# Attention in cross-shaped windows on one core: the kernel without the nine warming matmuls ahead of the first transposes

## The chip, the cores and the metric

The kernel runs on one NeuronCore of a Trainium2 chip. The metric is the device time of one execution in microseconds (us), the median of several runs; lower is better. The five engines are called as in the profile: PE (matrix multiply, with PEld for its weight loads), ACT (activation functions), DVE (vector), POOL (general purpose) and SP (it issues most transfers).

## The reference

The input is an image of 224 x 224 pixels with 96 channels. It is projected to q, k and v. The first 48 channels attend within horizontal stripes of 8 rows, the last 48 within vertical stripes of 8 columns, so there are 28 + 28 stripes of 1792 pixels each. The two halves are put side by side and projected once more.

```
qkv = einsum('bhwc,cd->bhwd', x, wqkv)            # 96 -> 3 * 96
ah  = softmax(einsum('bqc,bkc->bqk', qh, kh) * 48 ** -0.5)   # per horizontal stripe, 1792 x 1792
oh  = einsum('bqk,bkc->bqc', ah, vh)
av, ov = the same for the vertical stripes
o   = concat(oh, ov) over channels
return einsum('bhwc,cd->bhwd', o, wo)
```

## The kernel before

**Tiling.** Two stripes are worked on at a time; such a pair is called P, and there are 28 of them, 14 horizontal and 14 vertical. A pair has 4 query chunks (512, 512, 512 and 256 queries) and 14 key tiles of 128 keys. One unit of work is one chunk against one key tile for both stripes (two key tiles for the chunk of 256): PE writes 128 x 1024 scores into two PSUM banks (line 1015, `qk_op`), one engine turns them into exponentials, and PE multiplies these with V into the chunk's output (line 968, `pv_op`). Two matmuls that stand next to each other there use different parts of the array and run side by side, so matmuls are counted in pairs below.

**Who makes the exponentials.** Most units go to ACT: one activation of 128 x 1024 (line 1037), 1071 of them. The others go to DVE and POOL, which build the exponential from integer operations (lines 1075, 1088, 1090 and 1094).

**The order of the work.** Each engine has queues of operations, and the order in which a queue is served is written out by hand: `PLAN` holds one digit for each operation, and the digit names the queue that is served next. Digit 0 on PE is the queue `q_first`, the start of the kernel. Waits are semaphore waits that the planner puts ahead of an operation; every engine works its own list from first to last.

**The start**, which is where the change lies:

- ACT issues the transfer of the second stripe of pair 0 in natural layout (line 502, `x_nat`, into `Ph_sb`, which serves as scratch there), and then that of the weights `w_sb` (line 509). SP issues the transfer of the first stripe, transposed on its way (line 504, `x_tr`), and two more transposing ones for pair 1 (line 558).
- DVE clears `warm` (line 507) and other buffers and builds an identity matrix in `Ph_sb` (lines 513 to 521).
- PE runs `NWARM` matmuls of zeros (line 532): weights 128 x 128 and 512 columns, both from `warm`, into banks 0 to 3. Nobody reads the result. They wait for the clearing of `warm` alone.
- PE transposes the second stripe by 16 matmuls against the identity (line 647, `x_turn`, in four groups of four, numbered 0 to 3). DVE copies groups 0 and 2 to `xT_sb`, ACT groups 1 and 3 (line 652).
- PE projects K in four pieces (line 686) and Q of chunk 0 (lines 686 and 679); ACT and DVE copy them out (lines 705, 706 and 699), DVE adds up the sums of K and subtracts the mean (lines 713 and 719). PE then projects most of V (line 761) and Q of chunk 1, and starts the first scores (line 1015), for which it needs Q of chunk 0 and the first 256 keys from line 719. The first exponential on ACT follows.

The warming matmuls:

```
        for i in range(NWARM):
            first("pe", 0.427, lambda e, i=i: e.matmul(bank(i % 4)[:, :], lhsT=warm[:, 0:128], rhs=warm[:, :],
                                                       start=True, stop=True), [o_warm], mode="v")
```

## Time and profile before

| | |
|---|---|
| Median of 3 runs | 1008.08 us (1004.94 to 1011.19) |
| The profiled execution's own time | 1004.3 us |
| Its span, first to last instruction | 1002.5 us |
| ACT busy in it | 987.6 us (99%) |
| PE busy in it | 988.0 us (99%) |
| DVE and POOL busy in it | 938.5 us (94%) and 684.2 us (68%) |

Times within the profile are counted from the start of the span. The busy share of PE needs care: matmuls are pipelined and their ends are modelled, so that a PE shown as busy isn't necessarily at its peak. The clock column of the profile (PEclk) is the share of full speed that was granted to PE; what it says of the first microseconds is looked at below.

### The profile page before, as it was taken

What the parts mean: (1) busy time and instruction counts of PE and PEld (TensorE: products, weight loads), DVE (VectorE), ACT (ScalarE), POOL (GpSimd) and SP (SyncE); (2) the same over time, 40 slices, a digit from 0 to 9 for tenths busy, and PEclk for the clock granted to TensorE, in tenths of its full rate; (3) what the DMA queues carried; (4) which work ended last, traced back from release to release, by engine and by line L of the source; (5) the groups of instructions that cost most, each with busy time, mean ns of one, the idle gap of its engine ahead of it and who ended that gap; (6) DMA issues with size and microseconds to landing.
All of it is one profiled execution on the core that took longest, in us unless ns stands there. A gap on an engine that the chain in (4) does not pass through costs nothing.

```text
span 1002.5 us, 24560 instructions
## 1 busy us (share of the span) xinstructions
PE 988.0 (99%) x10211; PEld 385.9 (38%) x10211; DVE 938.5 (94%) x1573; ACT 987.6 (99%) x1080; POOL 684.2 (68%) x660
## 2 busy tenths in 40 slices
PE   8999999999999999999999999999999999999997
PEld 3433433343343334334334333433433443343342
DVE  8999999999999999999899999999999999999997
ACT  7999999999999999999999999999999999999997
POOL 3676766667677676777776776776676777677652
PEclk9999999999999999999999999999999999999999
DMA  5102120220112023011111122222122221222012
GB/s 110 39 2 38 38 32 8 38 38 1 39 39 32 8 38 38 2 36 25 27 29 32 25 46 50 54 52 44 34 41 52 53 54 39 52 52 40 13 36 50
DMA packets 164712, 36.92 MB, mean 37 GB/s; under 512 B 164488, under 2 KB 164488, under 8 KB 164600
## 3 DMA queue, kind: packets, MB, share of 16 engines
q1 hardware_dynamic: 163016, 34.80, 18.5%
q8 instruction: 80, 1.31, 0.5%
q10 hardware_dynamic: 1584, 0.55, 0.2%
q14 instruction: 32, 0.26, 0.1%
HBM read 0.44 MB, written 9.63 MB: 10 GB/s over the span
## 4 chain that ended last, share of the span: by engine, by line
ACT 70%; PE 29%; DVE 1%; issue 0%
ACT PT L1037 70%; PE ps L968 13%; PE ps L1015 11%; PE ps L686 2%; PE ps L761 1%; PE ps L843 1%; PE ps L532 0%; PE ps L809 0%; DVE OT_sb L931 0%; PE ps L647 0%; DVE out_sb L866 0%; DVE I_sb L1075 0%; DVE E_sb L1090 0%; DVE U_sb L1088 0%; PE ps L679 0%
## 5 line engine op out<-in xcount | busy, mean ns | idle before, releaser
L1037 ACT ACTIVATE PT<-ps 128x1024 bf16<-128x1024 f32 x1071 | 983.5, 1119 | 2.9 <-PE ps L1015 1.5
L1094 POOL TENSOR_TENSOR G_sb<-I_sb,U_sb 128x512 bf16<-128x512 bf16 x482 | 544.0, 1153 | 250.7 <-DVE E_sb L1090 225.3
L1015 PE MATMUL ps<-QT_sb,KT_sb 48*128 48x512 bf16 (+1 forms) x3136 | 463.0, 356 | 4.7 <-ACT PT L1037 3.0
L1075 DVE TENSOR_SCALAR I_sb<-ps 128x1024 int16<-128x1024 f32 x301 | 367.3, 1220 | 24.6 <-PE ps L1015 21.1
L968 PE MATMUL ps<-PT,V_sb 128*64 128x512 bf16 (+1 forms) x2422 | 363.8, 363 | 1.1 <-ACT PT L1037 1.0
L1015 PEld LDWEIGHTS ps<-QT_sb,KT_sb 48*128 48x128 bf16 x3136 | 123.2, 93 | 307.4 <-ACT PT L1037 223.7
L968 PEld LDWEIGHTS ps<-PT,V_sb 128*64 128x64 bf16 x2422 | 119.2, 109 | 122.5 <-issue 94.9
L968 PE MATMUL ps<-G_sb,V_sb 128*64 128x512 bf16 (+1 forms) x714 | 115.6, 356 | 0.0
L968 PE MATMUL ps<-E_sb,V_sb 128*64 128x512 bf16 (+1 forms) x714 | 109.9, 356 | 0.6 <-DVE OT_sb L931 0.2
L1088 DVE TENSOR_SCALAR U_sb<-I_sb 128x2048 int16<-128x2048 int16 (+1 forms) x161 | 109.2, 678 | 0.2
L859 POOL TENSOR_TENSOR out_sb<-tmp,Ph_sb 128x480 bf16<-128x480 f32 (+1 forms) x84 | 84.9, 1026 | 30.0 <-DVE E_sb L1090 10.7
L1090 DVE TENSOR_SCALAR E_sb<-I_sb 128x2048 int16<-128x2048 int16 (+1 forms) x161 | 104.9, 652 | 0.2 <-PE ps L968 0.2
L686 PE MATMUL ps<-xT_sb,w_sb 96*64 96x512 bf16 (+1 forms) x444 | 77.6, 367 | 0.9 <-ACT PT L1037 0.5
L931 DVE CAST OT_sb<-ps 128x512 bf16<-128x512 f32 x112 | 69.3, 619 | 5.9 <-PE ps L968 5.0
L706 DVE TENSOR_SCALAR_CACHE_REDUCE KT_sb<-ps 128x512 bf16<-128x512 f32 x110 | 67.8, 620 | 7.4 <-PE ps L686 6.8
L700 DVE TENSOR_SCALAR QT_sb<-ps 128x512 bf16<-128x512 f32 (+1 forms) x111 | 68.1, 619 | 5.2 <-PE ps L686 4.1
L766 DVE CAST V_sb<-ps 128x480 bf16<-128x480 f32 (+2 forms) x85 | 51.7, 611 | 3.1 <-PE ps L761 2.8
L968 PEld LDWEIGHTS ps<-G_sb,V_sb 128*64 128x64 bf16 x714 | 36.4, 108 | 47.3 <-issue 28.8
L720 POOL TENSOR_SCALAR KT_sb<-KT_sb,negmean 128x1792 bf16<-128x1792 bf16 x27 | 47.5, 1759 | 10.3 <-DVE E_sb L1090 6.2
L816 DVE TENSOR_TENSOR Ph_sb<-ps,rc 128x480 bf16<-128x480 f32 (+1 forms) x84 | 52.2, 622 | 2.1
L853 DVE TENSOR_TENSOR tmp<-ps,rc 128x480 f32<-128x480 f32 (+1 forms) x84 | 51.9, 618 | 2.2
L968 PEld LDWEIGHTS ps<-E_sb,V_sb 128*64 128x64 bf16 x714 | 33.9, 108 | 43.1 <-issue 21.1
(47 smaller groups left out, 324.4 us busy)
## 6 DMA issues: line engine op xcount, KB each, us to landing
out_dram<-out_sb SPq DMA_DIRECT2D x208, 42.0 KB, 2.1
xT_sb<-in_x_dram SPq DMA_TRANSPOSE x251, 2.4
out_dram<-out_sb SPq DMA_DIRECT2D x22, 24.0 KB, 1.9
Ph_sb<-in_x_dram ACTq DMA_DIRECT2D x1, 336.0 KB, 3.0
out_dram<-out_sb ACTq DMA_DIRECT2D x6, 24.0 KB, 1.9
wo_sb<-in_wo_dram SPq DMA_DIRECT2D x4, 9.0 KB
wo_sb<-one_sb SPq DMA_DIRECT2D x4, 0.0 KB
w_sb<-in_wqkv_dram ACTq DMA_DIRECT2D x1, 54.0 KB, 4.6
```

The source lines that it names most:

```text
L686: ins = e.matmul(bk[64 * w:64 * w + 64, 0:qs], lhsT=w_sb[0:C, wblk(P, kind), :], rhs=rhs, start=True, stop=True)
L700: return e.tensor_scalar(dst, src, QS, None, ALU.mult)
L706: return e.tensor_scalar(dst, src, 1.0, None, ALU.mult, ALU.add, accum_out=acc)
L859: return e.tensor_tensor(out_sb[b][:, k0:k0 + nk, ws[0], :], t, Ph_sb[:, k0:k0 + nk, j0 + ws[0], :], ALU.add)
L931: return e.tensor_copy(OT_sb[b][:, q0:q0 + qs], bk[:, 0:qs])
L968: return e.matmul(bank(k.bank)[64 * w:64 * w + 64, x0:x1], lhsT=lhs(w, kts[i])[p0:p1], rhs=rhs(w, i, qs)[p0:p1, x0:x1], start=(op.tok["fir ...
L1015: ins = e.matmul(bank(op.tok["s"][w])[:, i * qs:(i + 1) * qs], lhsT=KT_sb[b][64 * w:64 * w + C2, kt * 128:(kt + 1) * 128], rhs=QT_sb[b][64 ...
L1037: a.fn = lambda e: e.activation(PT[a.tok["p"]][:].rearrange("p (s n) -> p s n", s=2), two(q.tok["s"]), ACTF.Exp, scale=LN128)
L1075: return e.tensor_scalar(dst[:, at:at + 1024].rearrange("p (s n) -> p s n", s=2), two(src), 128.0 * ONE, 0.0, ALU.add, ALU.max)
L1088: f.fn = lambda e: e.tensor_scalar(U_sb[y()][:, 0:m], I_sb[y()][:, 0:m], M_FRAC, HALF, ALU.bitwise_and, ALU.bitwise_or)
L1090: x2.fn = lambda e: e.tensor_scalar(E_sb[x2.tok["l"]][:, 0:m], I_sb[y()][:, 0:m], M_EXP, E_LOW, ALU.bitwise_and, ALU.bitwise_or)
L1094: g.fn = lambda e: e.tensor_tensor(G_sb[x2.tok["l"]][:, i0:i1], I_sb[y()][:, i0:i1].bitcast(BF16), U_sb[y()][:, i0:i1].bitcast(BF16), ALU. ...
```

## The change

`NWARM` goes from 9 to 0, and nine zeros go from the head of PE's order, so that the nine matmuls of line 532 are no longer issued. PE's first instruction is now the first transpose of line 647. All other instructions of all engines, their order, their buffers and what they wait for are the same in both kernels; `warm` is still allocated and cleared.

```
 PLAN = {
     "pe": (
-        "00000000000000000066611216162164144116444216331216...
+        "00000000066611216162164144116444216331216...
...
-    NWARM, EARLY = 9, 256
+    NWARM, EARLY = 0, 256
```

More of the change, by code (lines that the diff above doesn't have):

```diff
@@ L34 @@
     "pe": (
-        "00000000000000000066611216162164144116444216331216431241641231431643441163446141541234133164412164412144312314"
+        "00000000066611216162164144116444216331216431241641231431643441163446141541234133164412164412144312314"
         "31631451431244144126143153121433146124153341143444131235144123414414126413311463643164154134143163124614412614"
```

## The prediction

> **What bounds the kernel now.** I read the page first (busy shares, chain), then ACT's waits, then the first 25 us of the timeline.

> ```profile
> PE 988.0 (99%) x10211; PEld 385.9 (38%) x10211; DVE 938.5 (94%) x1573; ACT 987.6 (99%) x1080; POOL 684.2 (68%) x660
> ACT 70%; PE 29%; DVE 1%; issue 0%
> L1037 ACT ACTIVATE PT<-ps 128x1024 bf16<-128x1024 f32 x1071 | 983.5, 1119 | 2.9 <-PE ps L1015 1.5
> 9.87 14.93 ACT L1037 ACTIVATE PT<-ps 128x1024 bf16<-128x1024 f32 x16 [0.71 <-PE ps L1015]
> ACT PT L1037 <- PE ps L968: 0.9, 4, 0.3
> ACT PT L1037 <- PE ps L1015: 0.8, 2, 0.4
> 979.10 16.51 ACT PT L1037 x18
> ```

> The third row is the group of ACT's exponentials, 1071 of them, 983.5 us busy. The fourth is from the timeline: the first starts at 9.87 us, and 16 take 14.93 us, so 0.93 us each. The two rows of waits are all that ACT waited between 12 us and the end: 1.7 us. The last row is from the chain in order of time: the last exponential ends at 979.10 + 16.51 = 995.61 us, and 6.9 us of tail follow to 1002.5.

> So the span is three terms: 9.87 us until the first exponential, 985.74 us of an ACT stream that hardly ever waits, and a tail of 6.9 us. The change touches the first term, and the second only if PE can't feed ACT. A microsecond saved or lost at the start is a microsecond of 1004; one per cent, about what a measurement of this kernel can tell from no change, is 10 us, more than the whole start. That fixes most of the answer before any detail.

> **What the start consists of.** These rows are from the timeline of the first 25 us:

> ```profile
> 0.73 1.33 SPq L504 DMA_TRANSPOSE xT_sb<-in_x_dram  x1
> 0.74 0.41 ACTq L502 DMA_DIRECT2D Ph_sb<-in_x_dram  x1
> 1.37 0.70 ACTq L509 DMA_DIRECT2D w_sb<-in_wqkv_dram  x1
> 1.19 4.02 PE L532 MATMUL ps<-warm 128*128 128x512 bf16 x9 [1.19 <-DVE warm L507]
> 3.19 0.76 DVE L521 TENSOR_TENSOR Ph_sb<-Ph_sb 32x32 bf16<-32x32 bf16 x4
> 5.00 1.70 PE L647 MATMUL ps<-Ph_sb 112*96 112x112 bf16 x16
> 6.00 0.54 ACT L652 ACTIVATE xT_sb<-ps 96x448 bf16<-96x448 f32 x1 [2.39 <-PE ps L647]
> 6.79 1.32 PE L686 MATMUL ps<-xT_sb,w_sb 96*64 96x512 bf16 x9
> 7.74 0.59 PE L679 MATMUL ps<-xT_sb,w_sb 96*64 96x256 bf16 x2
> 8.25 0.81 PE L761 MATMUL ps<-w_sb,xT_sb 96*64 96x48 bf16 x40
> 8.88 0.38 PE L686 MATMUL ps<-xT_sb,w_sb 96*64 96x512 bf16 x1
> 9.04 0.94 DVE L719 TENSOR_SCALAR KT_sb<-KT_sb,negmean 128x256 bf16<-128x256 bf16 x2
> 9.44 0.60 PE L1015 MATMUL ps<-QT_sb,KT_sb 48*128 48x512 bf16 x4
> ```

> and these from the transfers of the first 12 us, where the last number is us from issue to landing:

> ```profile
> Ph_sb<-in_x_dram ACTq DMA_DIRECT2D x1, 336.0 KB, 3.0
> w_sb<-in_wqkv_dram ACTq DMA_DIRECT2D x1, 54.0 KB, 4.6
> xT_sb<-in_x_dram SPq DMA_TRANSPOSE x3, 4.7
> ```

> **What the nine matmuls cost and bring.** They run from 1.19 to the transposes at 5.00, (5.00 - 1.19) / 9 = 0.423 us apart. What the transposes need is there earlier: the identity at 3.19 + 0.76 = 3.95, their input at 0.74 + 3.0 = 3.74. So the nine hold the transposes back by 5.00 - 4.03 = 0.97 us (0.08 us for the semaphore).

> What they bring is PE's clock.

> ```profile
> L532 PE MATMUL ps<-warm 128*128 128x512 bf16 x9 | 4.0, 631 | 1.2 <-DVE warm L507 1.2
> L647 PE MATMUL ps<-Ph_sb x16: 301/301/301, 5.0 to 6.4; 112*96 112x112 bf16 x16
> L686 PE MATMUL ps<-xT_sb,w_sb x11: 273/380/572, 6.8 to 13.3; 96*64 96x512 bf16 x9, 96*64 96x256 bf16 x2
> 6.79 0.57 PE L686 MATMUL ps<-xT_sb,w_sb 96*64 96x512 bf16 x2
> 11.86 0.39 PE L1015 MATMUL ps<-QT_sb,KT_sb 48*128 48x512 bf16 x2
> 12.78 0.61 PE L1015 MATMUL ps<-QT_sb,KT_sb 48*128 48x512 bf16 x4 [0.29 <-ACT PT L1037]
> 0.00:5.00 5.00, 3.81 (x9) 1.39 (x10) 2.68 (x15) 1.49 (x2) 2.04 (x13) 1.00 0.74 179
> 1000.00:1000.40 0.40, 0.00 (x0) 0.00 (x0) 0.00 (x0) 0.00 (x0) 0.00 (x0) 1.00 0.35 65
> 1000.50:1002.40 1.90, 0.00 (x0) 0.00 (x0) 0.00 (x0) 0.00 (x0) 0.00 (x0) 0.50 0.19 37
> ```

> One pair of 512 columns takes 0.39 us and two take 0.61 (the L1015 rows), so at 12 us a pair follows the one before after 0.22 us. The nine, also of 512 columns, stood 0.423 us apart: half speed. The 16 transposes all last 301 ns and stand (1.70 - 0.30) / 15 = 0.093 us apart, which is 1.2 columns per ns like the nine: half speed too. The first pair of K at 6.79 still lasts 0.57 us, while the median of that line is 380 ns. From the next pair on everything is quick. The clock column (third number from the right of the last three rows) reads 1.00 in the first 5 us, against these durations, so at the start I go by durations; at the end it does fall to 0.50 at about 1000.45, with PE idle since about 997. So full speed came at about 7.1 us, 5.9 us after PE's first matmul, and the nine warmed nothing but what comes after the transposes.

> [...]

> **The change step by step.**

> 1. *Transposes.* They start at 4.03 instead of 5.00, at half speed as before: their last ends 0.97 us earlier, at 5.73 instead of 6.70.
> 2. *K's first pair.* Before, it started at 6.79, right behind the transposes' end. Now it waits for w_sb, which lands at 1.37 + 4.6 = 5.97 (the transposed stripe lands at 0.73 + 4.7 = 5.43, and ACT's copy of group 1 ends at 6.54 - 0.97 = 5.57). With the same 0.08 us it starts at 6.05: 0.74 us gained, 0.23 of the 0.97 lost to w_sb.
> 3. *When the clock comes.* PE's first matmul moves from 1.19 to 4.03. With the same lag of 5.9 us full speed comes at 9.9 instead of 7.1, behind K, Q and V.
> 4. *K, Q and V at half speed.* One pair of 512 costs 0.21 us more. The rows have: two pairs of K with 512 columns (the first was slow before too), 0.21 each, one with 256, 0.11; Q of chunk 0, 0.21; Q of chunk 1, 0.21. That is 0.95 us. V's 40 matmuls of 48 columns take 0.81 us; whether columns or something else (weight loads, issue) sets their pace isn't seen, so half speed adds between nothing and 0.65 us; I take half, 0.33, as the row is between ends. Sum: 0.95 to 1.60, taken 1.28.
> 5. *First scores and first exponential.* The first pair of scores at half speed adds 0.18 us (0.57 against 0.39). PE gets there 1.28 - 0.74 = 0.54 us later than before; DVE's copy of K (9.04 + 0.30 for its first part, just ahead of the scores at 9.44) comes no later than before, as K's first three pairs are done 0.74, 0.53 and 0.32 earlier. So the first exponential starts 0.72 us later, at 10.6 instead of 9.87; by the bounds between 0.4 and 1.05 later.
> 6. *After it.* ACT needs a unit each 0.93 us. PE had idle time there (0.29 us ahead of the scores at 12.78), and full speed is due at 9.9, so I put nothing more down. If full speed came a further 3 us later, see the rival.

> DVE, POOL, SP and the transfers issue what they issued, and nothing else waits for line 532. The sum is +0.7 us: 1005.0 us against the profiled execution's 1004.3. The median of the runs shown is 3.8 us above that execution; I know no reason for the change to alter this, so 1008.1 + 0.7 = 1008.8 us.

> **The rivals.**

> *The clock comes as early as before, about 7.1 us or shortly after.* For it: the lag of 5.9 us is seen once, and PE is at work from 4.03 to 7.1 with a pause of only 0.3 us. Then the slow pairs of K are the first two or three, and 0.74 us minus 0.2 to 0.4 remain. DVE's chain ahead of the first scores allows about that. First exponential 0.4 us earlier: 1007.7 us. Against it: the 4 us of work from 1.19 to 5.2 hadn't brought it either. [...]

> *Full speed stays away: slower than before.* The place is PE behind the first exponential, where it waits for ACT now and then.

> ```profile
> 20.00:25.00 5.00, 5.00 (x40) 1.83 (x40) 4.96 (x11) 4.80 (x6) 2.96 (x3) 1.00 0.30 60
> PE ps L1015 <- ACT PT L1037: 1.3, 2, 1.0
> ```

> From 20 to 25 us PE issued 40 matmuls, 20 pairs: at 0.22 us that is 4.4 us of 5.0. At half speed they need 8.6 us, so 8.6 us at half speed lose 3.6, or 0.42 us per us. If PE's pauses there (up to 1.0 us, second row, from the first 30 us) kept the clock at half, 10 us would be lost in 24 us. That is the point from which it decides: full speed later than about 34 us gives 1018 us or more. Against it: with PE at half speed the pauses vanish, since it's then the bound, and constant work brought full speed within 6 us before. In a mild form, with full speed 3 us later than forecast, it costs 0.42 x 3 = 1.3 us: 1010.1 us.

> [...]

> *The change doesn't do what it says* can't be: line 532 is PE's first line, and nothing takes its place.

> **How the numbers follow.** The forecast gets 0.65, the early clock 0.15, the uncounted transposes 0.08, full speed staying away 0.06, and 0.06 remain for what I don't see in the scatter of 6 us between runs: 0.03 within 1%, 0.02 faster, 0.01 slower. Within 1%: 0.65 + 0.15 + 0.08 + 0.03 = 0.91; slower 0.06 + 0.01 = 0.07; faster 0.02. The predicted time is 1008.8 us. The mechanisms run from 1007.7 to 1010.1, but the runs before lie from 3.1 below to 3.1 above their median, so I take 1007.7 - 5 and 1010.1 + 4: 1002.7 to 1014.1 us.

> **What would show it right or wrong.** In the profile of the changed kernel the first L647 should stand at 4.0, the first L686 at 6.05 and the first L1037 at 10.3 to 10.9; L686 at 6 to 8 us should last about 570 ns throughout; ACT's waits behind the first exponential should stay near 1.7 us. A first L686 later than 6.2 would refute step 2; pairs 0.22 us apart before 9 us, step 3; a V of 0.81 us at half speed or of 1.4 would settle step 4. The answer as a whole is wrong if ACT's waits behind the first exponential grow by more than 5 us, or if the stream of 1071 takes another time each than 0.92.

## The result and the profile after

The changed kernel took 1013.5 us in the median of 20 runs (1007.66 to 1016.8), the kernel before 1006.16 us beside it (20 runs, 1003.33 to 1012.1). The ratio of the means is 1.0043 with a 95% interval of 1.0025 to 1.006: slower by about 4.3 us, within 1%. The medians lie further apart, 7.3 us, because the times of the changed kernel fall into two groups: 9 of the 20 lie at 1007.7 to 1009.4 us and 11 above 1013 us. In a later measurement (e5 below) the same two kernels gave 1.0022 (1.0004 to 1.004). The forecast was +0.7 us.

The profiled execution took 1014.34 us, with a span of 1012.5 us. Rows of the page, then ACT's waits for scores behind 12 us, as they were read before:

```profile
PE 993.3 (98%) x10202; PEld 386.9 (38%) x10202; DVE 939.6 (93%) x1573; ACT 989.0 (98%) x1080; POOL 685.2 (68%) x660
L1037 ACT ACTIVATE PT<-ps 128x1024 bf16<-128x1024 f32 x1071 | 984.8, 1116 | 11.3 <-PE ps L1015 9.8
PEclk9999999999999999999999999997999999999999
```

```profile
ACT PT L1037 <- PE ps L1015: 9.8, 13, 2.2
```

ACT's work is what it was (984.8 us against 983.5). It waits more: 9.8 us for scores in 13 places, where it was 0.8 us in 2. The clock row has one digit of 7 in the middle. The timeline of the start:

```profile
4.18 1.73 PE L647 MATMUL ps<-Ph_sb 112*96 112x112 bf16 x16 [4.18 <-DMA Ph_sb<-in_x_dram]
6.39 2.10 PE L686 MATMUL ps<-xT_sb,w_sb 96*64 96x512 bf16 x9 [0.48 <-DMA w_sb<-in_wqkv_dram]
8.28 1.56 PE L761 MATMUL ps<-w_sb,xT_sb 96*64 96x48 bf16 x37
9.64 0.61 PE L686 MATMUL ps<-xT_sb,w_sb 96*64 96x512 bf16 x1
10.80 1.04 PE L1015 MATMUL ps<-QT_sb,KT_sb 48*128 48x512 bf16 x4
11.45 1.94 ACT L1037 ACTIVATE PT<-ps 128x1024 bf16<-128x1024 f32 x2 [1.87 <-PE ps L1015]
17.74 1.00 PE L968 MATMUL ps<-PT,V_sb 128*64 128x512 bf16 x4
18.68 0.61 PE L1015 MATMUL ps<-QT_sb,KT_sb 48*128 48x512 bf16 x4
```

The chain in order of time has the transfer that K waited for, from its issue to its landing:

```profile
1.37 4.88 DMA w_sb<-in_wqkv_dram
```

The first exponential starts at 11.45 instead of 9.87. Two pairs of scores take 1.04 us at 10.80 and 0.61 at 18.68: PE stayed at half speed until 18.54 us. From there both chains run alike; this is the long piece of ACT in each, of the kernel before in the first fence and of the changed one in the second, and with the last piece:

```profile
25.18 19.36 ACT PT L1037 x21
```

```profile
28.90 19.36 ACT PT L1037 x21
984.53 21.09 ACT PT L1037 x23
```

Both pieces begin with the same exponential, the 17th. So the start cost 28.90 - 25.18 = 3.72 us in this execution. At the end the distance is 984.53 + 21.09 - 995.61 = 10.0 us. The other 6.3 us are lost in one place (up to the 732nd exponential the distance stays 3.72 us, and from the 746th on it is 10.0). The timeline there, and then the busy time by stretch, where the third number from the right is the granted clock:

```profile
687.30 0.43 PE L686 MATMUL ps<-xT_sb,w_sb 96*64 96x512 bf16 x2 [1.84 <-issue]
689.17 1.02 ACT L1037 ACTIVATE PT<-ps 128x1024 bf16<-128x1024 f32 x1 [2.21 <-PE ps L1015]
```

```profile
18.60:687.50 668.90, 663.83 (x7012) 257.47 (x7012) 623.57 (x1031) 666.87 (x727) 473.21 (x445) 1.00 0.18 32
687.60:697.70 10.10, 10.10 (x55) 3.31 (x51) 7.11 (x13) 6.11 (x6) 3.09 (x4) 0.50 0.24 45
```

PE paused 1.84 us ahead of a K projection of a vertical pair, and right behind the pause its clock fell to half for 10.2 us. The kernel before ran the same projection without a pause:

```profile
681.58 0.39 PE L686 MATMUL ps<-xT_sb,w_sb 96*64 96x512 bf16 x2
```

Is that the change's doing, or does it happen to both kernels? And why did full speed come at 18.5 us, not at 9.9?

### The profile page after: what moved, and what is told of

It is laid out like the page before. It is cut to its first block, busy times and chain, and to the rows that moved or that the text cites. A ratio compares the mean times of both kernels' runs of the same rounds, so it can differ in the third digit from the quotient of the medians.

```text
span 1012.5 us, 24542 instructions
## 1 busy us (share of the span) xinstructions
PE 993.3 (98%) x10202; PEld 386.9 (38%) x10202; DVE 939.6 (93%) x1573; ACT 989.0 (98%) x1080; POOL 685.2 (68%) x660
## 4 chain that ended last, share of the span: by engine, by line
ACT 69%; PE 29%; DVE 1%; DMA 0%; issue 0%
ACT PT L1037 69%; PE ps L968 13%; PE ps L1015 12%; PE ps L686 2%; PE ps L761 1%; PE ps L843 1%; DMA w_sb<-in_wqkv_dram 0%; PE ps L809 0%; DVE OT_sb L931 0%; PE ps L679 0%; DVE out_sb L866 0%; DVE I_sb L1075 0%; DVE E_sb L1090 0%; DVE U_sb L1088 0%; DVE KT_sb L706 0%
## 5 line engine op out<-in xcount | busy, mean ns | idle before, releaser
L1037 ACT ACTIVATE PT<-ps 128x1024 bf16<-128x1024 f32 x1071 | 984.8, 1116 | 11.3 <-PE ps L1015 9.8
L1015 PE MATMUL ps<-QT_sb,KT_sb 48*128 48x512 bf16 (+1 forms) x3136 | 466.5, 358 | 4.2 <-ACT PT L1037 2.5
L968 PE MATMUL ps<-PT,V_sb 128*64 128x512 bf16 (+1 forms) x2422 | 366.1, 364 | 1.1 <-ACT PT L1037 1.0
L1015 PEld LDWEIGHTS ps<-QT_sb,KT_sb 48*128 48x128 bf16 x3136 | 123.1, 93 | 309.8 <-ACT PT L1037 222.7
L968 PEld LDWEIGHTS ps<-PT,V_sb 128*64 128x64 bf16 x2422 | 119.8, 109 | 123.8 <-issue 96.2
L968 PE MATMUL ps<-G_sb,V_sb 128*64 128x512 bf16 (+1 forms) x714 | 116.2, 358 | 0.0
L968 PE MATMUL ps<-E_sb,V_sb 128*64 128x512 bf16 (+1 forms) x714 | 110.4, 357 | 0.5 <-DVE OT_sb L931 0.2
L859 POOL TENSOR_TENSOR out_sb<-tmp,Ph_sb 128x480 bf16<-128x480 f32 (+1 forms) x84 | 85.1, 1028 | 32.6 <-DVE E_sb L1090 10.7
L686 PE MATMUL ps<-xT_sb,w_sb 96*64 96x512 bf16 (+1 forms) x444 | 79.2, 373 | 3.1 <-issue 1.8
L706 DVE TENSOR_SCALAR_CACHE_REDUCE KT_sb<-ps 128x512 bf16<-128x512 f32 x110 | 67.9, 620 | 10.6 <-PE ps L686 10.1
L968 PEld LDWEIGHTS ps<-G_sb,V_sb 128*64 128x64 bf16 x714 | 36.5, 108 | 47.5 <-issue 28.4
L720 POOL TENSOR_SCALAR KT_sb<-KT_sb,negmean 128x1792 bf16<-128x1792 bf16 x27 | 47.6, 1762 | 10.3 <-DVE E_sb L1090 6.2
L968 PEld LDWEIGHTS ps<-E_sb,V_sb 128*64 128x64 bf16 x714 | 34.0, 108 | 43.2 <-issue 21.6
## 6 DMA issues: line engine op xcount, KB each, us to landing
Ph_sb<-in_x_dram ACTq DMA_DIRECT2D x1, 336.0 KB, 3.4
```

Source lines behind the costliest of these rows:

```text
L686: ins = e.matmul(bk[64 * w:64 * w + 64, 0:qs], lhsT=w_sb[0:C, wblk(P, kind), :], rhs=rhs, start=True, stop=True)
L706: return e.tensor_scalar(dst, src, 1.0, None, ALU.mult, ALU.add, accum_out=acc)
L859: return e.tensor_tensor(out_sb[b][:, k0:k0 + nk, ws[0], :], t, Ph_sb[:, k0:k0 + nk, j0 + ws[0], :], ALU.add)
L968: return e.matmul(bank(k.bank)[64 * w:64 * w + 64, x0:x1], lhsT=lhs(w, kts[i])[p0:p1], rhs=rhs(w, i, qs)[p0:p1, x0:x1], start=(op.tok["fir ...
L1015: ins = e.matmul(bank(op.tok["s"][w])[:, i * qs:(i + 1) * qs], lhsT=KT_sb[b][64 * w:64 * w + C2, kt * 128:(kt + 1) * 128], rhs=QT_sb[b][64 ...
L1037: a.fn = lambda e: e.activation(PT[a.tok["p"]][:].rearrange("p (s n) -> p s n", s=2), two(q.tok["s"]), ACTF.Exp, scale=LN128)
```

## The experiments

**Seven warming matmuls (e1).** They end when the transposes' input lands.

```
-    NWARM, EARLY = 0, 256
+    NWARM, EARLY = 7, 256      # and 7 zeros more at the head of PE's order
```

> Seven warming matmuls instead of nine: at 0.427 us each from 1.19 they end at 4.18, when the transposes' input has landed, so they hold nothing back. Theory (window): full speed comes at the end of a fixed stretch of 3.41 us in which PE's matmuls stream nearly all the time; PE then streams from 1.19 to 5.7 without a break, so in most executions full speed comes before 8.5 us; first exponential at 9.0 to 9.9, lower cluster of times within 1 us of the kernel before. Rival (lateness): what costs 3.7 us at the start is w_sb landing and the order, not the clock; then this kernel is like the changed one, +3 to +4 us.

1004.81 us (12 runs) beside 1006.39 of the kernel before (35 runs); 0.9993 (0.9969 to 1.0017). Lateness falls: `w_sb` came as late here (K starts at 6.35), yet K's nine matmuls took 1.13 us, against 2.10 in the changed kernel.

```profile
4.15 1.70 PE L647 MATMUL ps<-Ph_sb 112*96 112x112 bf16 x16
6.35 1.13 PE L686 MATMUL ps<-xT_sb,w_sb 96*64 96x512 bf16 x9 [0.50 <-DMA w_sb<-in_wqkv_dram]
10.43 0.61 PE L1015 MATMUL ps<-QT_sb,KT_sb 48*128 48x512 bf16 x4 [0.99 <-ACT PT L1037]
```

```profile
6.10:12.80 6.70, 5.17 (x86) 2.62 (x87) 5.84 (x16) 5.40 (x10) 0.00 (x0) 1.00 0.49 104
12.90:16.20 3.30, 3.30 (x15) 0.70 (x12) 2.80 (x4) 2.08 (x3) 0.42 (x1) 0.50 0.00 0
16.30:20.00 3.70, 3.69 (x31) 1.32 (x31) 2.57 (x5) 3.63 (x4) 3.70 (x4) 1.00 0.58 128
```

The first exponential came at 9.26, but the lead was lost again: full speed was taken away from 12.9 to 16.2 us, one stretch, and ACT waited 3.9 us for scores in all. In the 3.4 us ahead of that drop PE had paused 0.99 us and otherwise ran few columns: 5 pairs of scores (0.22 us each) and 16 short V matmuls, about 1.4 us of 3.4. That fits the second half of the theory: full speed went behind a thin stretch. The kernel before has the same pauses (0.99 and 0.29 us, ahead of 11.04 and 12.78) and kept full speed in its trace. Its stretches lie otherwise: full speed came at 7.17 us there, so that the end of a stretch, 3.41 us later at 10.59, cuts the long pause (10.05 to 11.04) in two. Here the drop at 12.9 puts the ends of the stretches at about 9.45 and 6.04 us, so that the long pause (9.44 to 10.43) lies in one.

**One more matmul ahead of K (e2).**

```
+                if f is x_turn and args[0] == 3:    # behind the last group of transposes
+                    first("pe", 0.427, lambda e: e.matmul(bank(0), lhsT=warm[:, 0:128], rhs=warm[:, :], start=True, stop=True), ...)
```

> As the one with seven warming matmuls, and one more of 512 columns between the transposes and K's first pair, where PE idles 0.4 to 0.7 us for w_sb. Theory (window): PE then streams from 1.19 to about 6.2 with no break, so full speed comes by 8.0 us in nearly all executions; first exponential 0.3 to 0.8 us before that of the kernel before; median 0.5 us below it. Rival (lateness): the one more matmul delays K by up to 0.2 us and nothing is gained: +3 to +4 us like the changed kernel.

1004.75 us (12 runs), 0.9993 (0.997 to 1.0015): lateness falls again, but neither the forecast gain of 0.5 us over the kernel before nor one over the kernel with seven is shown. In the profiled execution ACT waited 4.0 us for scores in 6 places, as in that with seven (3.9 in 6), so the loss behind the start was still there.

**Forty short matmuls (e3), and three long ones (e4).**

```
-    e.matmul(bank(i % 4)[:, :], lhsT=warm[:, 0:128], rhs=warm[:, :], ...)          # NWARM = 0
+    e.matmul(bank(i % 4)[:, 0:48], lhsT=warm[:, 0:128], rhs=warm[:, 0:48], ...)    # NWARM = 40
```

> Forty warming matmuls of 48 columns (weights 128x128 each time) instead of nine of 512: PE has instructions from 1.19 to about 5, but streams less than half of the time. Theory (window): that does not count as dense, full speed comes as late as in the changed kernel or later (first K pairs 570 ns, full speed behind 11 us), and time is 3 to 5 us above the kernel before. Rival (any instruction counts): full speed at 4.6 to 8 us as in the kernel before, time within 1 us of it.

1008.61 us (1007.17 to 1009.53, 10 runs), a ratio of 1.0017 (0.9997 to 1.0036). The profile is as the theory had it (K's nine matmuls took 2.10 us, and two pairs of scores at 10.79 us still 1.04), the time is less clear: its median is 2.2 us above that of the kernel before, where 3 to 5 were expected. And the run didn't test what was meant: the forty ended at 1.19 + 1.78 = 2.97 us, so PE paused before the transposes.

```profile
1.19 1.78 PE L532 MATMUL ps<-warm 128*128 128x48 bf16 x40 [1.19 <-DVE warm L507]
```

`NWARM = 3`, with three zeros more:

> Three warming matmuls, from 1.19 to 2.47, then PE idles until the transposes at 4.1. Theory (window): the three share no window with enough else, so nothing is gained over the changed kernel: +3 to +4 us over the kernel before in the lower cluster. Rival (amount of work counts, each matmul brings its share): three ninths of the loss are won back, +2 to +2.5 us.

1008.18 us (1007.21 to 1009.61, 10 runs), against 1006.39; the ratio, 1.0016 (0.9994 to 1.0038), doesn't tell the theory from the rival, since runs of the kernel before lose time elsewhere too. Its own fastest lies 4.2 us above the fastest of the kernel before (1003.05), and in its trace K ran at half speed (eight matmuls in 1.71 us) and the first exponential came at 11.60 us, as late as in the changed kernel. So in this trace three ninths of the work bought nothing.

**110 matmuls of 8 columns (e9)**, the test that the forty missed.

```
+    e.matmul(bank(i % 4)[:, 0:8], lhsT=warm[:, 0:128], rhs=warm[:, 0:8], ...)      # NWARM = 110
```

> 110 warming matmuls of 8 columns (weights 128x128 each time), to fill 1.19 to about 4.1 us with instructions that stream little; the forty of 48 columns ended at 2.95, since they too ran at 48 columns in 40 ns, and so tested only a pause. Theory (streaming counts): full speed late, first exponential at 11 to 11.7, fastest execution above 1007. Rival (any instruction counts as busy): PE is busy from 1.19 to 5.7 as with seven warming matmuls, full speed by 8 us, first exponential near 9.3, fastest execution below 1004.5.

1008.42 us (1007.63 to 1009.76, 10 runs) against 1005.24 (25 runs): 1.0021 (1.0011 to 1.0031). As the theory had it, the fastest is above 1007; the rival's 1004.5 isn't reached. The first exponential came at 10.98 us.

```profile
1.19 3.10 PE L532 MATMUL ps<-warm 128*128 128x8 bf16 x110 [1.19 <-DVE warm L507]
4.15 1.71 PE L647 MATMUL ps<-Ph_sb 112*96 112x112 bf16 x16
6.29 2.10 PE L686 MATMUL ps<-xT_sb,w_sb 96*64 96x512 bf16 x9 [0.43 <-DMA w_sb<-in_wqkv_dram]
10.55 0.61 PE L1015 MATMUL ps<-QT_sb,KT_sb 48*128 48x512 bf16 x4
```

```profile
13.80:20.50 6.70, 6.61 (x28) 1.95 (x28) 4.08 (x8) 4.94 (x6) 2.56 (x3) 0.50 0.01 2
20.60:30.00 9.40, 9.38 (x71) 3.17 (x72) 8.53 (x16) 8.27 (x9) 4.77 (x5) 1.00 0.48 98
```

PE is busy from 1.19 to 5.86 us by the profile, just like with seven long matmuls, and its transposes start at the same 4.15. Yet K ran at half speed (2.10 us, not 1.13). So having instructions wasn't enough here: the 110 streamed 880 columns in all, the seven 3584. Full speed was there at 10.55 us (two pairs of scores in 0.61 us), gone again from 13.8 to 20.5, and then stayed. The three drops seen so far last 3.4, 6.8 and 10.2 us: one, two and three stretches. The drop here didn't come behind an idle stretch: PE was busy for 2.21 of the 3.30 us from 10.4 to 13.7.

**Scores computed again in the pauses (e7, e11).** The second and fourth unit's scores go four times and twice into the same banks, which changes no value; a pause behind the first exponential becomes dense.

```
-                for i, kt in enumerate(kts):
+                for i, kt in list(enumerate(kts)) * op.again:     # qk_op; again is 4 for unit 1, 2 for unit 3, else 1
```

> Seven warming matmuls, one more ahead of K, and the second and fourth unit of scores computed four times and twice into the same banks, so that PE streams in the pauses behind the first exponential. Theory (window): a window that streams less than about half takes full speed away again (seen with seven warming matmuls, 12.9 to 16.3 us); with the pauses filled the drop is gone: lower cluster at 1002.5 to 1004, and none of the times 1 to 2.5 us above it that a drop costs. Rival (the drop has another cause): the profile or the spread shows it still, and the median is that of the kernel with seven and one, 1004.7.

With seven warming matmuls and the one ahead of K: 1003.75 us, all 12 runs between 1003.13 and 1004.6, against 1006.46 (35 runs, 1003.6 to 1011.64): 0.9967 (0.9954 to 0.9981). This is faster than the kernel before, and than the changed kernel beside it (1008.65, e5 below).

```profile
9.05 1.25 PE L1020 MATMUL ps<-QT_sb,KT_sb 48*128 48x512 bf16 x10
9.48 7.50 ACT L1043 ACTIVATE PT<-ps 128x1024 bf16<-128x1024 f32 x8 [0.62 <-PE ps L1020]
```

```profile
7.20:1000.00 992.80, 982.59 (x10192) 382.81 (x10188) 933.81 (x1556) 985.31 (x1076) 682.27 (x647) 1.00 0.19 36
```

(Lines behind 640 are moved by up to 6 there.) With the repeats on the kernel before alone:

> Nine warming matmuls as before, with the second and fourth unit of scores computed four times and twice. Theory (window): in a part of the executions of the kernel before, full speed is taken away again behind the first exponential, which costs 1 to 2.5 us; with the pauses filled that is gone: median about 1004, spread 1003.3 to 1005. Rival (the kernel with seven, one and repeats is faster by its earlier first exponential alone): no change against before, 1006.4.

1004.26 us (1003.55 to 1005.1, 10 runs) against 1005.24 (25 runs): 0.9985 (0.9973 to 0.9998). So the repeats help by themselves, which fits a kernel before that loses full speed behind its start in many executions; none of these was profiled, so the place is inferred from what the repeats change. One stretch at half speed is 3.41 x 0.5 / 1004 = 0.0017 of the granted share. Of the 35 runs of the kernel before beside e7, the 19 with a share of 0.995 to 0.997 (one or two stretches) took 1005.1 to 1007.9 us, and 9 with 0.998 or more took 1003.6 to 1004.8 but for one (1006.2); in e7 all 12 have 0.997 to 0.999. In this trace full speed came so early that the transposes ran in it: 16 in 0.95 us instead of 1.70.

```profile
4.87 0.95 PE L648 MATMUL ps<-Ph_sb 112*96 112x112 bf16 x16
```

**The drop in the middle: the changed kernel again (e5), and without half of its stores (e10).**

> The changed kernel once more, beside the others. Theory (window): each execution loses 3 to 4.5 us at the start, so its fastest time is 1007 or more, while the kernel before has half of its executions below 1006.5. Executions with a stall in the middle come on top, 4 to 6 us each, and these owe nothing to the change: they occur in both kernels. Rival (the change also makes the stalls more frequent): half of its executions above 1012 here too, against one in ten of the kernel before.

1008.65 us (1007.46 to 1013.12, 10 runs); one of ten above 1012, so half of the executions, as the rival had it, isn't seen here. The profiled execution has the pause ahead of K's pair too, 1.38 us, but its clock stays:

```profile
686.51 0.41 PE L686 MATMUL ps<-xT_sb,w_sb 96*64 96x512 bf16 x2 [1.38 <-issue]
```

```profile
18.30:1004.00 985.70, 975.70 (x10093) 379.84 (x10091) 925.59 (x1539) 978.49 (x1066) 682.27 (x647) 1.00 0.19 35
```

Without half of the stores:

```
-                                for w in range(2):     # stores of a vertical pair: 16
+                                for w in range(1):     # 8
```

> The changed kernel without the stores of the second stripe of each vertical pair (but for the last pair): half of those outputs are not written, 8 stores in place of 16 per pair on SP. Theory: the stall at 685 us is K's first pair waiting for a load behind the 16 stores; with 8 it is gone in all executions (the step of 0.8 to 2.3 us at the 732nd exponential too), and the spread shrinks to the start's: 1006 to 1008.5 us. Rival (the drop in the middle comes by itself): some executions at 1012 and above remain.

1007.36 us (1006.81 to 1008.37, 10 runs). The same K pair has no pause at all:

```profile
685.23 0.41 PE L968 MATMUL ps<-PT,V_sb 128*64 128x256 bf16 x4
685.48 0.38 PE L686 MATMUL ps<-xT_sb,w_sb 96*64 96x512 bf16 x2
```

So the pause is K waiting for `x`, whose loads stand behind the stores in SP's queue. The trace of the changed kernel has the same: SP issues 16 stores from 671.51 us on and the next two loads only at 682.66 and 683.96; the last piece lands at 687.21, and K starts at 687.30. (Half of the stores are also half of the bytes written, so e10 alone doesn't tell the queue from the traffic.) That no run was above 1008.4 proves less, since the kernel before had none above 1008.7 beside it either.

The start of this kernel is that of the changed one, and its trace shows another course of it: full speed came at 9.98 us and was lost again for two stretches.

```profile
10.00:13.30 3.30, 2.31 (x29) 0.74 (x26) 2.42 (x4) 2.49 (x3) 0.00 (x0) 1.00 0.02 5
13.50:20.10 6.60, 6.38 (x28) 1.95 (x28) 4.20 (x8) 4.93 (x6) 2.34 (x3) 0.50 0.00 0
```

**Loads ahead of stores**, on the changed kernel (e6) and on the best one (e8).

```
-        sp_out, sp_in = (pl.stream("sp", i) for i in range(2))
+        sp_out, sp_in = (pl.stream("sp", 1 - i) for i in range(2))
```

> The changed kernel, with the transposing loads of x ahead of the stores on SP whenever both are ready (all other engines in the same order). Theory (stall by load): the stall in the middle is PE waiting for a load that stood behind 16 stores, and the drop of the clock follows from it; with the loads ahead no execution has it: all within 1007 to 1009.5 us, clock share 0.998 or more. Rival (the clock drops by itself, whatever SP does): executions at 1012 and more with a share of 0.993 remain.

> The kernel with seven, one and repeated scores, and SP's loads ahead of its stores. If both theories hold, neither drop is left: all executions within 1002 to 1004.5 us, median 1003.2, 3 us below the kernel before. If the stall in the middle has another cause, a fifth to a half of the executions stay at 1008 to 1012.

Both missed: 1012.35 us (1009.9 to 1015.69, 10 runs), and 1008.62 (1005.62 to 1010.9, 12 runs), slower than without the edit. Six of the ten lie above 1012, the sign that the rival had given. But the stall moved. In the first of them (waits, timeline, busy time by stretch):

```profile
POOL out_sb L859 <- DMA out_dram<-out_sb: 3.2, 1, 3.2
```

```profile
790.78 0.41 PE L968 MATMUL ps<-G_sb,V_sb 128*64 128x256 bf16 x4 [1.79 <-POOL G_sb L1094]
```

```profile
792.20:798.80 6.60, 6.60 (x33) 1.96 (x31) 5.73 (x10) 5.27 (x6) 3.96 (x4) 0.50 0.24 48
```

Now the stores are late: POOL waits 3.2 us for one to free its buffer, its products come late, PE pauses 1.79 us, and the clock falls again, for 6.8 us. In e8 the granted share of the profiled execution is 0.996, where it was 0.999 in e7, a difference of about two stretches. So in both traces shown with a drop in the middle, the changed kernel's and that of e6, it comes 0.3 and 1.4 us behind the end of a pause of 1.8 us, and the pause has two different causes. That speaks against "by itself"; the cure was the wrong one.

## Why the prediction was right or wrong

The class was right: the change stays within 1%, since the whole start is short. That 1013.5 lies in the range is luck: the mechanisms ended at 1010.1, the rest up to 1014.1 was room for scatter, and the median stands there because more than half of the runs belong to the upper group, which no step foresaw (the drop in the middle, as far as the one profile shows). The base was off too: 1008.1 was the median of 3 runs, and 20 runs gave 1006.16. And the runs tell less than the one per cent that was assumed: the interval here is 0.25% to 0.6%. The likeliest change was not met: +0.7 us against +4.3 and +2.2 in two measurements.

The signs that the prediction had named for itself say the same. ACT's waits behind 12 us grew from 1.7 to 9.8 + 0.9 = 10.7 us, where a growth of more than 5 was to mean that the answer as a whole is wrong; 5.4 of them belong to the drop in the middle. By the steps:

1. *Transposes* (step 1) at 4.03, were 4.18: their input landed a little later. *K's first pair* (step 2) at 6.05, was 6.39, later than the 6.2 that was to refute the step: `w_sb` took 4.88 us instead of 4.6, and K started 0.14 behind it, not 0.08. The gain was 6.79 - 6.39 = 0.40 us, not 0.74. Right in kind, and the size varies: in e5, e6 and e10, which start like the changed kernel, K's first pair stood at 6.04, 6.09 and 6.29.
2. *When the clock comes* (step 3) is the step that failed. I moved the one lag of 5.9 us along with PE's first matmul, and got 9.9; it was 18.5. Full speed came 5.98 us after PE's first matmul in the kernel before and 14.36 us after it in the changed one, both times at the end of a stretch that streamed densely. By the estimate given below, the five stretches of the changed kernel that ended at 4.9, 8.3, 11.7, 15.1 and 18.5 us streamed 0.20, 0.80, 0.74, 0.57 and 0.87 of the time, and only the last brought full speed. The forecast 9.9 can occur: in e10 full speed came at 9.98 us. But it was taken away again one stretch later, from 13.4 to 20.2, and the start still cost 3.9 us. So the forecast also failed in taking for granted that full speed, once there, stays.
3. *K, Q and V at half speed* (step 4): from K's start to the first scores it was 10.80 - 6.39 = 4.41 us against 9.44 - 6.79 = 2.65, so 1.76 against my 1.28, and above the upper bound of 1.60. V took 9.64 - 8.28 = 1.36 us against 8.88 - 8.25 = 0.63, so 0.73: the upper end, 0.65, was the right one. Q of chunk 1 cost 10.80 - 9.64 = 1.16 against 9.44 - 8.88 = 0.56, 0.60 where I had 0.21; the last matmul ahead of the scores lasts 0.71 us there and 0.42 before.
4. *First exponential* (step 5) 1.58 us later, forecast 0.72; at 11.45 it is outside the 10.3 to 10.9 given.
5. *After it* (step 6) I put nothing; it was 3.72 - 1.58 = 2.1 us, PE at half speed failing to feed ACT until 18.5. The rival's price for this, 0.42 us for each us at half speed, gives 0.42 x (18.5 - 11.45) = 3.0 us. So "full speed stays away" was the true rival in its mild form, at a chance of 0.06; it put full speed 3 us later than forecast, and here it was 8.6.

The chance of 0.08 went to transposes that don't count as work for the clock. No run shows such a thing, and they aren't needed to explain the lag: e11 ran 16 of them at full speed (0.95 us instead of 1.70), and by the estimate below the stretch that brought full speed in the kernel before streamed 0.91 of the time, but 0.48 without the transposes, while stretches of 0.74 to 0.84 didn't bring it in the traces before and after. The early clock (first exponential ahead of 9.87) came true only where warming matmuls were kept.

The 6.3 us in the middle of the profiled execution aren't shown to be the change's doing. The pause exists in several kernels, with an early start (1.41 us in e1, 1.42 in e2, 0.94 in e7) and with a late one (1.84, and 1.38 in e5, but none in e9). Times that high occurred in both: above 1011 us were 11 of 20 and 1 of 10 runs of the changed kernel, and 6 of 20, 3 of 35, 5 of 35 and none of 25 of the kernel before. None of the latter was profiled, so that they have the same cause is likely, not shown. Whether a later start makes SP miss its moment more often, and why the best kernel had none in 12, stays open. The two measurements of the change differ in the number of such runs, and so in their ratios.

That the clock followed how much PE streamed, not how long it was busy, is shown by e1 against e9: PE is busy from 1.19 to about 5.86 us in both, and K's nine matmuls took 1.13 and 2.10 us. What share of a stretch PE streamed is an estimate, from the start and the columns of every matmul in the traces before and after and the rates seen there (512 columns in 0.217 us at full speed, in 0.427 at half), with overlaps counted once and the stretches laid out by the changes of the clock. The stretches that brought full speed streamed 0.91 (the kernel before, up to 7.17 us), 0.87 and 0.92 (the changed one, up to 18.54 and 697.80 us); 0.84 and less didn't. The one that lost it in the middle streamed 0.35; those that kept it 0.57 or more, but for one near the end of the kernel before (0.38, from 993.6 to 997.0 us). At the end of the two kernels, stretches of 0.00 and 0.12 lost it. How sharp these lines are isn't shown. Of the pauses ahead of the drops, 1.84 us (the changed kernel) and 1.79 us (e6) were followed by the loss; 1.38 us (e5) was not.

## What to carry to other kernels

Warming matmuls must hand over: here they paid where PE then stayed dense until full speed came (K in 1.13 us in e1, 2.10 in e9), and part of it was lost again in the first pauses of the pipeline (half speed from 12.9 to 16.2 us in e1). There, harmless repeats of real matmuls in those pauses brought 0.15% on the kernel before, and 0.33% together with warming that held nothing back. Look for PE's pauses anywhere in a kernel near PE's limit: here pauses of 1.84 and 1.79 us were paid twice, the second time as 10.2 and 6.8 us at half speed, and one of 1.38 us (e5) left the clock at full speed. And one lag read from one trace is a draw, not a constant: with the same start, full speed came at 18.54 us in the changed kernel's trace and at 9.98 in that of e10.

## What the runs showed that was not expected

- PE that is busy by the profile from 1.19 to 5.86 us with matmuls of 8 columns and the transposes doesn't have full speed for K (e9): K took 2.10 us there and 1.13 behind dense ones (e1).
- Full speed was lost again 3.4 us after its coming (e9: V and Q of chunk 1 still slow at 9.5 to 10.3 us, full at 10.34, gone at 13.75, back at 20.57).
- The kernel before had time to gain behind its own start: 8 matmuls more, all repeats, took it from 1005.24 to 1004.26 us (e11).
